# Joint attention block on one core: the image values multiplied key tile by key tile, narrow products in one bank, fourth token tile last

## The chip, the cores and the metric

The kernel runs on one core of a Trainium2 chip. The metric is the device time of one execution in microseconds (us); lower is better. A core has five engines that run side by side and wait for each other through semaphores: TensorE (matmuls; PE in the profile, its weight loads PEld), VectorE (DVE), ScalarE (ACT), GpSimd (POOL) and SyncE (SP), whose queue issues most of the loads (DMAs).

## What is computed

A joint attention block over 2 batches of 256 image tokens and 32 text tokens, width D = 1152, bfloat16. Cut to what matters here (the text side has the same form with its own weights):

```python
mod = (silu(c) @ wmod_img).reshape(B, 6, 1, D)
sh, sc, ga = mod[:, 0], mod[:, 1], mod[:, 2]
h = layernorm(x_img) * (1 + sc) + sh
q, k, v = split(h @ wqkv_img)
p = softmax(concat(qt, q) @ concat(kt, k).T * D ** -0.5)
out = x_img + ga * ((p @ concat(vt, v))[image rows] @ wo_img)
```

## The kernel before, in words

The 512 image tokens are four tiles of 128 rows (`NIT`, two to a batch, `TPB`), and D is nine key tiles of 128 (`KT`). The order of the work on every engine is the order in which the program is written (`tc.manual_schedule()`), so a wait of one instruction holds all that stand behind it on its engine. PSUM has eight banks: seven in the pool `ps_mm`, which are reused in turn, and one in `ps_sm`.

The part that the change rewrites is the value stage, from the first scale columns to the first q product:

- **Loads** (lines 92 to 118), all from SyncE's queue. The scale weights `w_sc_i` come in four chunks of columns, the value weights `w_v_i` in chunks of key tiles, both cut as `KC` says: (0,2), (2,4), (4,6), (6,9). The order is x tiles 0 and 1, scale chunk 0, x tile 2, value chunk 0, x tile 3, then scale and value chunks by turns, key tile 6 and key tiles 7 and 8 of the values on their own, then the shift and q weights in thirds (`K3`).
- **Normalising** (lines 164 to 180): VectorE's statistics of a tile, ScalarE's square root, VectorE's normalised rows `xn_i`.
- **Transposes** (`x_transposes`, line 193): nine per tile on TensorE into two PSUM tiles; ScalarE copies them to `hT_i` (`evac_low`, `evac_high`, lines 202 and 205) or, for the key tiles whose scale is known by then, scales them on the way (`evac_scaled`, line 198).
- **Scale** (`mod_scale`, line 210): 18 or 27 two-column matmuls per chunk, to which one engine adds 1 (line 219 or 221). `apply_mod` then multiplies `hT_i` in place by VectorE (0, line 229), GpSimd (1, line 234) or ScalarE (2, line 238).
- **Value products without the shift** (`v_part`, line 250). Each tile has two 512-wide halves, each with a bank of its own, and a 128-wide rest. `v_block` takes units and chunks by turns; seven of the eight halves are done so. The eighth is done behind them (line 401), and the rests last, two tiles to a bank (`v_rest`, line 350). `evac` empties a bank by VectorE and ScalarE in turn (lines 159 and 161).
- **Shift** of the image rows: `rows_for_cols` makes strips of the shift (lines 374 and 378), `select_cols` turns them into columns (390, 392), `cols_out` copies them out (395, 397), `apply_mod` adds them to `hT_i` after the value products have read it. The first 18 of the narrow rests stand in front of `select_cols`, the other 18 behind it.

What the values lack is put right later: VectorE multiplies the value weights by the shift (`shift_products`, lines 446 and 448), which goes through `shift_high`, `shift_low` (461) and `shift_strip` (468, 471).

Behind it, `qk_img` (line 486) makes q and then k for all 512 image tokens in 512-wide products: the first three column tiles as a group with the key tile as the outer loop, each later one on its own. Hooks put other work between them; in k these are the text side's normalising, its strips, its columns (`all_cols`, line 526), transposes (539) and the sums on VectorE (540, 542) that the text products (552) wait for. Then come scores, softmax, the attention output and the output projection (821).

Of the kernel before, what the change touches and what calls it, by code (L numbers as in the profile page):

```python
# [8 lines left out]
ACT = mybir.ActivationFunctionType  # L9
# [5 lines left out]
def kernel(  # L15
# [54 lines left out]
    def w_view(src):  # L70
        return src.rearrange("(kt p) n -> p kt n", p=P)
# [20 lines left out]
    def load_x(i):  # L92
        nc.sync.dma_start(x_i[:, i, :], xi_t[:, i, :])  # L93

    def load_sc(ch):
        k0, k1 = KC[ch]
        nc.sync.dma_start(w_sc_i[:, :, k0 * P:k1 * P], w_view(wmod_img)[:, :, D + k0 * P:D + k1 * P])

    def load_v(ch):
        k0, k1 = KC[ch]  # L100
        nc.sync.dma_start(w_v_i[:, k0:k1, :], w_view(wqkv_img)[:, k0:k1, 2 * D:3 * D])

    load_x(0)
    load_x(1)
    load_sc(0)
    load_x(2)
    load_v(0)
    load_x(3)
    for ch in range(1, len(KC)):
        load_sc(ch)  # L110
        if ch < len(KC) - 1:
            load_v(ch)
# [69 lines left out]
    xn_i = act.tile([P, NIT, D], bf, tag="A")  # L182
    hT_i = act.tile([P, KT, B * NI], bf, tag="Bt")

    mod_i = const.tile([P, 2 * KT, B], f32, name="mod_img")

    def x_transposes(i, n0=5):
        tps = (ps_mm.tile([P, n0, P], bf, tag="mm", name="tp"),
               ps_mm.tile([P, KT - n0, P], bf, tag="mm", name="tp") if n0 == 5 else
               ps_sm.tile([P, KT - n0, P], bf, tag="sm", name="tp"))  # L190
        for kt in range(KT):
            tp = tps[0][:, kt, :] if kt < n0 else tps[1][:, kt - n0, :]
            nc.tensor.transpose(tp, xn_i[:, i, kt * P:(kt + 1) * P], ident[:])  # L193
        return tps + (n0,)

    def evac_scaled(i, tps, n):
        for kt in range(n):
            nc.scalar.activation(hT_i[:, kt, i * P:(i + 1) * P], tps[0][:, kt, :], ACT.Identity,  # L198
                                 scale=mod_i[:, KT + kt, i // TPB:i // TPB + 1])

    def evac_low(i, tps, n):
        nc.scalar.copy(hT_i[:, n:tps[2], i * P:(i + 1) * P], tps[0][:, n:tps[2], :])

    def evac_high(i, tps):
        nc.scalar.copy(hT_i[:, tps[2]:KT, i * P:(i + 1) * P], tps[1][:])

    def mod_cols(wt, out_ps, j0, j1):
        for j in range(j0, j1):
# [1 line left out]
                nc.tensor.matmul(out_ps[:, j - j0, :], lhsT=wt[:, kt, j * P:(j + 1) * P], rhs=sT[:, kt, :],  # L210
                                 start=(kt == 0), stop=(kt == KT - 1))

    def mod_scale(ch, eng, own=True):
        k0, k1 = KC[ch]
        pool, tag = (ps_sm, "sm") if own else (ps_mm, "mm")
# [25 lines left out]

    vacc = {}

    def v_part(i, half, ch):
        k0, k1 = KC[ch]
        if ch == 0:
            vacc[i, half] = ps_mm.tile([P, VW], f32, tag="mm", name=f"va{i}{half}")
        ps = vacc[i, half]
        for kt in range(k0, k1):
            nc.tensor.matmul(ps[:], lhsT=hT_i[:, kt, i * P:(i + 1) * P], rhs=w_v_i[:, kt, half * VW:(half + 1) * VW],  # L250
                             start=(kt == 0), stop=(kt == KT - 1))
        if k1 == KT:
            evac(v_i[:, i, half * VW:(half + 1) * VW], ps[:])


    def v_block(units, chs):
        for ch in chs:
            for (i, half) in units:
                v_part(i, half, ch)

    warm(4)
    silu_c()
# [3 lines left out]
    def stats_of(i, k0, k1):  # L266
        lns[i] = ln_stats(x_i[:, i, :], P, k0, k1, lns.get(i))
# [10 lines left out]
    std_of(1)  # L278
    out_of(0)
    mod_scale(0, "act")  # L280
    tp0 = x_transposes(0)
    evac_scaled(0, tp0, 2)
    out_of(1)
    warm(1)
    tp1 = x_transposes(1, KT - 1)
    stats_of(2, 0, NCH)
    evac_scaled(1, tp1, 2)
    evac_low(0, tp0, 2)
    std_of(2)
    evac_high(0, tp0)  # L290
    evac_high(1, tp1)
    stats_of(3, 0, 1)
    out_of(2)
    v_block([(0, 0), (0, 1), (1, 0), (1, 1)], [0])
    evac_low(1, tp1, 2)
    tps = x_transposes(2, KT - 1)
    stats_of(3, 1, NCH)
    evac_scaled(2, tps, 2)
    std_of(3)
    mod_scale(1, "dve", own=False)  # L300
    for n, kt in enumerate(range(*KC[1])):
        apply_mod(kt, 0, 2, False, n)
    evac_low(2, tps, 2)
    evac_high(2, tps)
    v_block([(2, 0), (2, 1)], [0])
    out_of(3)
    for kt in range(*KC[1]):
        apply_mod(kt, 2, 3, False, 0)
    v_block([(0, 0), (0, 1)], [1])
    tps = x_transposes(3, KT - 1)  # L310
    evac_high(3, tps)
    evac_scaled(3, tps, 4)
    evac_low(3, tps, 4)
    v_block([(1, 0), (1, 1)], [1])
    mod_scale(2, "dve")
    for kt in range(*KC[2]):
        apply_mod(kt, 0, 2, False, 0)
        apply_mod(kt, 2, 4, False, 1)
    v_block([(2, 0), (2, 1)], [1])
    v_block([(3, 0)], [0, 1])  # L320
    v_i = act.tile([P, NIT, D], bf, tag="A")
    SEVEN = [(i, half) for i in range(NIT) for half in range(2)][:7]
    for (i, half) in SEVEN[:5]:
        v_part(i, half, 2)
    mod_scale(3, "dve")
    for b in range(B):
        for n, kt in enumerate(range(*KC[3])):
            apply_mod(kt, b * TPB, (b + 1) * TPB, False, (n + b) % 3)
    for (i, half) in SEVEN[5:]:
        v_part(i, half, 2)  # L330
    for (i, half) in SEVEN:
        v_part(i, half, 3)
# [5 lines left out]
    v_t = act.tile([P, VW], bf)  # L338
    v_t8 = act.tile([NTT, P], bf)
# [6 lines left out]
    def v_rest(i0, i1):  # L346
        ps = ps_mm.tile([P, TPB, P], f32, tag="mm")
        for kt in range(KT):
            for i in range(i0, i1):
                nc.tensor.matmul(ps[:, i - i0, :], lhsT=hT_i[:, kt, i * P:(i + 1) * P], rhs=w_v_i[:, kt, NM:D],  # L350
                                 start=(kt == 0 and i == i0), stop=(kt == KT - 1 and i == i1 - 1))
        return ps

    def v_rest_out(i0, i1, ps):
        evac(v_i[:, i0:i1, NM:D], ps[:])

    NGG = 4
    RC = 2 * P
# [40 lines left out]
    ps = ps_mm.tile([P, VW], f32, tag="mm")  # L399
    for kt in range(KT):  # L400
        nc.tensor.matmul(ps[:], lhsT=hT_i[:, kt, 3 * P:4 * P], rhs=w_v_i[:, kt, VW:NM], start=(kt == 0), stop=(kt == KT - 1))  # L401
    evac(v_i[:, 3, VW:NM], ps[:])
# [12 lines left out]
    w_k_i = load_w(wqkv_img, D, K3)  # L415
    w_sh_t = load_w(wmod_txt, 0)
# [57 lines left out]
        evac(g_sb[:], gps[:], "act")  # L474
        return g_sb

    def qk_img(wq, blk, hooks):

        groups = [(0, 3)] + [(j, j + 1) for j in range(3, KT)]
        for (j0, j1) in groups:  # L480
            if j0 in hooks:
                hooks[j0]()
            pss = [ps_mm.tile([P, B * NI], f32, tag="mm", name="qkps") for _ in range(j0, j1)]
            for kt in range(KT):
                for j in range(j0, j1):
                    nc.tensor.matmul(pss[j - j0][:], lhsT=wq[:, kt, j * P:(j + 1) * P], rhs=hT_i[:, kt, :],  # L486
                                     start=(kt == 0), stop=(kt == KT - 1))
# [36 lines left out]
        nc.scalar.activation(junk[:], eps_t[:], ACT.Exp)  # L524

    def all_cols():
        ctp = ps_sm.tile([P, 2, NCOL + B], f32, tag="sm")
        for k, rows in enumerate((strips["tsh"], strips["tsc"])):
            select_cols(rows, ctp[:, k, :])
        for k in range(2):  # L530
            cols_out(mod_t[:, k, :, :], ctp[:, k, :], float(k))

    def txt_transposes():
        pick = ident[:].rearrange("p (t r) -> p r t", r=P // NTT)[:, 0, :]
# [23 lines left out]
        all_cols()  # L558
        txt_transposes()

    qk_img(w_k_i, 1, hooks={3: txt_norm, 6: row_strips, 7: cols_and_transposes, 8: lambda: qk_txt(w_q_t, 0)})
    qk_txt(w_k_t, 1)


# [334 lines left out]
```

## Time and profile before

| | us |
|---|---|
| median of 3 runs | 116.68 (116.31 to 116.77) |
| the profiled execution | 116.51 |
| its span, first to last instruction | 114.5 |
| TensorE busy | 108.8 (95%) |
| VectorE, ScalarE, GpSimd busy | 75.0, 39.7, 27.6 |
| value stage, first scale column to first q product | 7.30 to 31.88 |
| q and k for the image, L486 | from 31.88, 162 products |
| DMA | 40.87 MB, 357 GB/s on average, about 410 from 20 us on |

In the timeline's rows the columns are: start, length, engine, line, operation, what it writes and reads, how often, and in brackets the engine's idle time before it with what ended it. Matmuls are pipelined, so that a row of them goes on for a little after the next row has started; the step from one start to the next is what a matmul costs. The granted clock of TensorE was 0.998 of full speed over the span.

### The profile page before, as it was taken

The page shows a single profiled execution, that of the slowest core. Times are in us where ns is not written, and L with a number is a line of the kernel's source. Part 1 is how long each engine was busy: PE and PEld are TensorE (multiplying, and loading weights), DVE is VectorE, ACT ScalarE, POOL GpSimd, SP SyncE. Part 2 cuts the span into 40 slices and gives each one's busy share as a digit, 9 for nine tenths or more (in the row PEclk, how much of TensorE's full clock was granted, in tenths as well). Part 3 has the DMA queues.
Part 4 walks back from the last instruction along what each step waited for, and adds up shares of the span by engine and source line. Part 5 has one row for each costly group of instructions (what it writes and reads, how often), then busy time and mean ns, then how long its engine had stood idle before and what let it go on. Part 6 is the DMA issues. An engine that isn't in the chain of part 4 may idle for free.

```text
span 114.5 us, 2919 instructions
## 1 busy us (share of the span) xinstructions
PE 108.8 (95%) x1230; PEld 64.7 (56%) x1230; DVE 75.0 (66%) x150; ACT 39.7 (35%) x93; POOL 27.6 (24%) x60
## 2 busy tenths in 40 slices
PE   5978999999999999999999999999999999999990
PEld 1344564544954444444447658787697566567560
DVE  1698920353399999999999760227656803998770
ACT  2729760342380630730009924025646700001000
POOL 7000103550050000000000051501540560899200
PEclk9999999999999999999999999999999999999999
DMA  3999999999999999999999999999999999962042
GB/s 81 315 346 355 372 383 398 411 412 411 408 407 412 405 416 401 412 412 411 412 411 411 410 405 411 404 389 399 411 408 403 409 410 398 388 273 102 26 163 69
DMA packets 22775, 40.87 MB, mean 357 GB/s; under 512 B 1311, under 2 KB 6571, under 8 KB 22763
## 3 DMA queue, kind: packets, MB, share of 16 engines
q1 hardware_dynamic: 21680, 39.64, 90.9%
q0 software_dynamic: 608, 0.88, 2.1%
q10 hardware_dynamic: 475, 0.18, 0.6%
q8 instruction: 9, 0.15, 0.5%
q14 instruction: 3, 0.02, 0.1%
HBM read 39.36 MB, written 1.34 MB: 356 GB/s over the span
## 4 chain that ended last, share of the span: by engine, by line
PE 87%; DMA 6%; SPq 2%; DVE 1%; issue 0%
PE qkps L486 31%; PE ps L821 16%; PE va L250 11%; DMA x_i<-in_x_img_dram 6%; PE aps L729 5%; PE ps L552 4%; PE sps L585 4%; PE gps L374 3%; PE ops L839 2%; PE ps L350 2%; PE ps L401 2%; PE ps L660 2%; SPq L93 1%; PE mps L210 1%; PE gps L794 1%; PE tp L193 1%
## 5 line engine op out<-in xcount | busy, mean ns | idle before, releaser
L486 PE MATMUL qkps<-hT_i,t 128*128 128x512 bf16 x162 | 35.6, 379 | 0.0
L486 PEld LDWEIGHTS <-t 128*128 128x128 bf16 x162 | 15.6, 98 | 18.3 <-issue 0.2
L448 DVE SCALAR_TENSOR_TENSOR sacc<-w_v_i,mod_img,sacc 128x1152 f32<-128x1152 bf16 x16 | 22.7, 1418 | 0.5
L821 PE MATMUL ps<-t,aT 128*128 128x384 bf16 x99 | 16.4, 326 | 0.0
L250 PE MATMUL va<-w_v_i,hT_i 128*128 128x512 bf16 x63 | 14.6, 379 | 0.5 <-DMA w_v_i<-in_wqkv_img_dram 0.5
L821 PEld LDWEIGHTS <-aT 128*128 128x128 bf16 x117 | 11.0, 98 | 6.8 <-issue 0.5
L827 DVE TENSOR_TENSOR tmp<-ps,gb 128x384 bf16<-128x384 f32 x11 | 6.1, 551 | 6.1 <-DMA gb<-mod_scratch 4.9
L250 PEld LDWEIGHTS <-hT_i 128*128 128x128 bf16 x63 | 5.8, 97 | 7.2 <-ACT hT_i L198 0.8
L805 POOL TENSOR_TENSOR w_og<-t,gb 128x384 bf16<-128x384 bf16 x9 | 8.8, 1006 | 4.5 <-PE ps L821 4.5
L507 POOL TENSOR_SCALAR svn<-svr 128x128 bf16<-128x128 bf16 x1 | 0.3, 298 | 32.8 <-ACT svr L156 32.8
L168 DVE BATCH_NORM_STATS2 stats<-x_i 128x6 f32<-128x384 bf16 x12 | 5.9, 543 | 2.9 <-DMA x_i<-in_x_img_dram 2.9
L436 ACT ACTIVATE qT<-qkps 128x512 bf16<-128x512 f32 x9 | 4.9, 596 | 6.4 <-PE qkps L486 6.4
L452 ACT CAST shi<-sacc 128x1152 bf16<-128x1152 f32 x2 | 2.3, 1152 | 13.7 <-DVE sacc L448 13.7
L142 PE MATMUL wps<-wz 128*128 128x512 bf16 x16 | 5.6, 499 | 1.2 <-DVE wz L127 1.2
L234 POOL TENSOR_SCALAR hT_i<-hT_i,mod_img 128x256 bf16<-128x256 bf16 x5 | 2.5, 510 | 15.9 <-ACT rstd L175 9.2
L742 DVE TENSOR_SCALAR aT<-aps,sv 128x288 bf16<-128x288 f32 (+2 forms) x11 | 4.3, 457 | 1.9 <-PE aps L729 1.9
L552 PEld LDWEIGHTS <-t 128*128 128x128 bf16 x162 | 4.9, 98 | 0.7 <-issue 0.5
L156 DVE CAST kT<-qkps 128x512 bf16<-128x512 f32 x3 | 2.1, 686 | 4.7 <-PE qkps L486 4.7
L552 PE MATMUL ps<-hT_t,t 128*128 128x64 bf16 x162 | 5.0, 193 | 0.0
L828 DVE TENSOR_TENSOR o<-tmp,x_i 128x384 bf16<-128x384 bf16 x11 | 4.7, 428 | 0.4
L744 ACT ACTIVATE aT<-aps,sv 128x288 bf16<-128x288 f32 (+2 forms) x11 | 4.0, 468 | 2.2 <-PE aps L729 2.2
L729 PE MATMUL aps<-pT,v_i 128*128 128x288 bf16 (+2 forms) x44 | 4.8, 264 | 0.0
(166 smaller groups left out, 148.0 us busy)
## 6 DMA issues: line engine op xcount, KB each, us to landing
t<-in_wmod_txt_dram SPq DMA_DIRECT2D x3, 2592.0 KB, 21.9
t<-in_wqkv_img_dram SPq DMA_DIRECT2D x6, 864.0 KB, 13.1
t<-in_wqkv_txt_dram SPq DMA_DIRECT2D x2, 2592.0 KB, 18.4
t<-in_wmod_img_dram SPq DMA_DIRECT2D x3, 864.0 KB, 11.6
w_home<-in_wmod_img_dram SPq DMA_DIRECT2D x1, 2592.0 KB, 14.7
t<-in_wqkv_txt_dram SPq DMA_DIRECT2D x3, 864.0 KB, 14.2
t<-in_wo_img_dram SPq DMA_DIRECT2D x1, 2592.0 KB, 17.8
t<-in_wo_txt_dram SPq DMA_DIRECT2D x3, 864.0 KB, 15.6
```

Of the source, the lines that this page charges most:

```text
L142: nc.tensor.matmul(ps[:], lhsT=wz[:, 0:P], rhs=wz[:], start=True, stop=True)
L168: nc.vector.bn_stats(stats[0:np_, k, :], x_ap[:, k * CH:(k + 1) * CH])
L250: nc.tensor.matmul(ps[:], lhsT=hT_i[:, kt, i * P:(i + 1) * P], rhs=w_v_i[:, kt, half * VW:(half + 1) * VW], start=(kt == 0), stop=(kt == K ...
L436: nc.scalar.mul(out_ap, in_ap, SCALE)
L448: nc.vector.scalar_tensor_tensor(saccs[b][:], w_v_i[:, kt, :], ap, saccs[b][:], op0=ALU.mult, op1=ALU.add)
L486: nc.tensor.matmul(pss[j - j0][:], lhsT=wq[:, kt, j * P:(j + 1) * P], rhs=hT_i[:, kt, :], start=(kt == 0), stop=(kt == KT - 1))
L552: nc.tensor.matmul(ps[:, j - j0, :], lhsT=wq[:, kt, j * P:(j + 1) * P], rhs=hT_t[:, kt, :], start=(kt == 0), stop=(kt == KT - 1))
L729: nc.tensor.matmul(bank[:, off:off + c1 - c0], lhsT=lhsT, rhs=rhs, start=(first[id(bank)] == n), stop=(final[id(bank)] == n))
L805: nc.gpsimd.tensor_mul(w_og[:, dt, 0:CH], w_o_i[:, dt, NG0:D], gb[:, B - 1, NG0:D])
L821: nc.tensor.matmul(ps[:, 0:cw], lhsT=aT[:, dt, t0:t0 + P], rhs=rhs, start=(dt == DTS[0]), stop=(dt == DTS[-1]))
L827: nc.vector.tensor_mul(tmp[:, 0:cw], ps[:, 0:cw], gb[:, b, cs])
L828: nc.vector.tensor_add(o[:, cs], tmp[:, 0:cw], x_i[:, i, cs])
```

## The change

- Value weights are loaded one key tile to a DMA (`load_v`), key tiles 7 and 8 still together. The fourth x tile's load moves to the place before the last scale chunk.
- `x_transposes` becomes `x_heads` (the first two key tiles; those of tiles 0 and 1 share a bank) and `x_tails` (the other seven). ScalarE scales the heads, key tile by key tile; the tails are copied by ScalarE, three key tiles of tile 1 by VectorE. The filler matmul `warm(1)` goes.
- `v_part` becomes `v_wide` and `v_narrow`. The narrow products of all four tiles share one bank, `van`, from the start, and stand between the wide ones; `v_row` does both halves of one tile and one key tile.
- The first three tiles' products follow the value rows as they come. The fourth tile's statistics, rows and transposes come late (`last_transposes`, VectorE scales on the way out), and its products come last. Its second half runs across `select_cols`, where the rests stood.
- `xn_i` shares the space of q, no longer that of `v_i`.
- q's first group has five column tiles, k's still three.
- The text columns go to two PSUM tiles; those of the shift are copied by ScalarE (`cols_copy`), those of the scale by VectorE, first.

The diff, cut to its core:

```diff
     def load_v(ch):
-        k0, k1 = KC[ch]
-        nc.sync.dma_start(w_v_i[:, k0:k1, :], w_view(wqkv_img)[:, k0:k1, 2 * D:3 * D])
+        for kt in range(*KC[ch]):
+            nc.sync.dma_start(w_v_i[:, kt:kt + 1, :], w_view(wqkv_img)[:, kt:kt + 1, 2 * D:3 * D])
...
     load_v(0)
-    load_x(3)
     for ch in range(1, len(KC)):
+        if ch == len(KC) - 1:
+            load_x(3)
         load_sc(ch)
...
+    def x_heads(tiles):
+        tp = ps_mm.tile([P, len(tiles), H, P], bf, tag="mm", name="tph")
+        for n, i in enumerate(tiles):
+            for kt in range(H):
+                nc.tensor.transpose(tp[:, n, kt, :], xn_i[:, i, kt * P:(kt + 1) * P], ident[:])
+        return tp
...
+    def x_tails(i):
+        pool, tag = (ps_mm, "mm") if i < TPB else (ps_sm, "sm")
+        tp = pool.tile([P, KT - H, P], bf, tag=tag, name="tp")
+        for kt in range(H, KT):
+            nc.tensor.transpose(tp[:, kt - H, :], xn_i[:, i, kt * P:(kt + 1) * P], ident[:])
+        return tp
...
+    def v_narrow(i, k0, k1):
+        if i == 0 and k0 == 0:
+            vacc["n"] = ps_mm.tile([P, NIT, P], f32, tag="mm", name="van")
+        for kt in range(k0, k1):
+            nc.tensor.matmul(vacc["n"][:, i, :], lhsT=hT_i[:, kt, i * P:(i + 1) * P], rhs=w_v_i[:, kt, NM:D],
+                             start=(i == 0 and kt == 0), stop=(i == NIT - 1 and kt == KT - 1))
+
+    def v_row(i, kt):
+        v_wide(i, 0, kt, kt + 1)
+        v_wide(i, 1, kt, kt + 1)
+
+    def last_transposes(k0, k1):
+        i = NIT - 1
+        b = i // TPB
+        tp = ps_sm.tile([P, k1 - k0, P], bf, tag="sm", name="tp")
+        for kt in range(k0, k1):
+            nc.tensor.transpose(tp[:, kt - k0, :], xn_i[:, i, kt * P:(kt + 1) * P], ident[:])
+        nc.vector.tensor_mul(hT_i[:, k0:k1, i * P:(i + 1) * P], tp[:],
+                             mod_i[:, KT + k0:KT + k1, b:b + 1].to_broadcast([P, k1 - k0, P]))
...
     out_of(1)
-    warm(1)
...
+    heads = x_heads((0, 1))
+    tails = [x_tails(i) for i in range(TPB)]
     stats_of(2, 0, NCH)
+    for kt in range(H):
+        for i in range(TPB):
+            head_scaled(heads, i, i, kt)
+    tail_out(0, tails[0], H, H + 3)
     std_of(2)
+    tail_out(1, tails[1], H, H + 3, on_vector=True)
+    tail_out(0, tails[0], H + 3, KT)
+    tail_out(1, tails[1], H + 3, KT)
     out_of(2)
+    for kt in range(*KC[0]):
+        for i in range(TPB):
+            v_row(i, kt)
+    for i in range(TPB):
+        v_narrow(i, *KC[0])
+    head2 = x_heads((2,))
+    tail2 = x_tails(2)
+    mod_scale(1, "dve", ps_mm, "mm")
...
+    v_wide(2, 0, *KC[0])
+    v_narrow(2, *KC[0])
+    v_wide(2, 1, *KC[0])
...
+    for kt in range(*KC[1]):
+        for i in range(TPB):
+            v_row(i, kt)
     mod_scale(2, "dve")
...
+    for i in range(TPB):
+        v_narrow(i, *KC[1])
+    for kt in range(*KC[1]):
+        v_row(2, kt)
+    v_narrow(2, *KC[1])
+    stats_of(3, 0, NCH)
+    std_of(3)
+    out_of(3)
+    k0, k1 = KC[2]
+    for i in range(3):
+        v_row(i, k0)
+    for i in range(TPB):
+        v_row(i, k0 + 1)
+    v_row(2, k0 + 1)
+    v_narrow(0, k0, k1)
     mod_scale(3, "dve")
...
+    for i in range(1, 3):
+        v_narrow(i, k0, k1)
+    last_transposes(0, KT - 1)
+    k0 = KC[3][0]
+    for i in range(3):
+        v_row(i, k0)
+        v_narrow(i, k0, k0 + 1)
+    last_transposes(KT - 1, KT)
+    for i in range(3):
+        for half in range(2):
+            v_wide(i, half, k0 + 1, KT)
+        v_narrow(i, k0 + 1, KT)
+    v_wide(3, 0, 0, KT)
+    v_narrow(3, 0, KT)
...
     shr = rows_for_cols(w_sh_i, "shr")
     cps = ps_sm.tile([P, NCOL + B], f32, tag="sm")
-    v_rest_out(TPB, NIT, v_rest(TPB, NIT))
+    v_wide(3, 1, 0, 5)
     select_cols(shr, cps)
     cols_out(mod_i[:, 0:KT, :], cps, 0.0)
-    vr = v_rest(0, TPB)
+    v_wide(3, 1, 5, KT, out=False)
...
-    v_rest_out(0, TPB, vr)
+    v_wide_out(3, 1)
+    evac(v_i[:, :, NM:D], vacc["n"][:])
...
-    qk_img(w_q_i, 0, hooks={5: lambda: shift_high(0)})
+    qk_img(w_q_i, 0, 5, hooks={5: lambda: shift_high(0)})
...
-        ctp = ps_sm.tile([P, 2, NCOL + B], f32, tag="sm")
-        for k, rows in enumerate((strips["tsh"], strips["tsc"])):
-            select_cols(rows, ctp[:, k, :])
-        for k in range(2):
-            cols_out(mod_t[:, k, :, :], ctp[:, k, :], float(k))
+        ctps = (ps_mm.tile([P, NCOL + B], f32, tag="mm", name="ctp"), ps_sm.tile([P, NCOL + B], f32, tag="sm", name="ctp"))
+        for ctp, rows in zip(ctps, (strips["tsh"], strips["tsc"])):
+            select_cols(rows, ctp)
+        cols_out(mod_t[:, 1, :, :], ctps[1], 1.0)
+        cols_copy(mod_t[:, 0, :, :], ctps[0])
```

More of the change, by code (lines that the diff above doesn't have):

```diff
@@ L180, in ln_apply, with head_scaled, tail_out @@
         nc.vector.tensor_scalar(out_ap, x_ap, mv[0:np_, 0:1], rstd[0:np_, :], op0=ALU.subtract, op1=ALU.mult)
-    xn_i = act.tile([P, NIT, D], bf, tag="A")
     hT_i = act.tile([P, KT, B * NI], bf, tag="Bt")
+    v_i = act.tile([P, NIT, D], bf, tag="A")
+    v_t = act.tile([P, VW], bf)
+    v_t8 = act.tile([NTT, P], bf)
+    xn_i = act.tile([P, NIT, D], bf, tag="Q")
     mod_i = const.tile([P, 2 * KT, B], f32, name="mod_img")
[L187 to L205, printed above, removed]
+    H = KC[0][1]
+    def x_heads(tiles):
[4 more added lines that the diff above has]
+        return tp
+    def head_scaled(tp, n, i, kt):
+        nc.scalar.activation(hT_i[:, kt, i * P:(i + 1) * P], tp[:, n, kt, :], ACT.Identity,
+                             scale=mod_i[:, KT + kt, i // TPB:i // TPB + 1])
+    def x_tails(i):
[4 more added lines that the diff above has]
+        return tp
+    def tail_out(i, tp, k0, k1, on_vector=False):
+        (nc.vector.tensor_copy if on_vector else nc.scalar.copy)(hT_i[:, k0:k1, i * P:(i + 1) * P], tp[:, k0 - H:k1 - H, :])
     def mod_cols(wt, out_ps, j0, j1):
@@ L211, in mod_cols, with mod_scale @@
                                  start=(kt == 0), stop=(kt == KT - 1))
[L213 removed]
+    def mod_scale(ch, eng, pool=ps_sm, tag="sm"):
         k0, k1 = KC[ch]
[L215 removed]
         mps = pool.tile([P, KT, B], f32, tag=tag)
@@ L242, with v_wide @@
     vacc = {}
-    def v_part(i, half, ch):
-        k0, k1 = KC[ch]
-        if ch == 0:
+    def v_wide(i, half, k0, k1, out=True):
+        if k0 == 0:
             vacc[i, half] = ps_mm.tile([P, VW], f32, tag="mm", name=f"va{i}{half}")
@@ L251, in v_part, with v_wide_out @@
                              start=(kt == 0), stop=(kt == KT - 1))
[L252 to L259, printed above, removed]
+        if k1 == KT and out:
+            v_wide_out(i, half)
+    def v_wide_out(i, half):
+        evac(v_i[:, i, half * VW:(half + 1) * VW], vacc[i, half][:])
+    def v_narrow(i, k0, k1):
[15 more added lines that the diff above has]
+                             mod_i[:, KT + k0:KT + k1, b:b + 1].to_broadcast([P, k1 - k0, P]))
     warm(4)
@@ L344 @@
     pxs = [act.tile([P, 2, B, NT], bf, name=f"px_{q}") for q in range(TPB)] + [act.tile([P, 2, B, NT], bf, name="px_t")]
[L346 to L355, printed above, removed]
     NGG = 4
@@ L397, in cols_out, with cols_copy @@
         nc.vector.tensor_scalar_add(dst[:, KT - 1, :], cps[:, NCOL:NCOL + B], add)
[L399 to L402, printed above, removed]
+    def cols_copy(dst, cps):
+        nc.scalar.copy(dst[:, 0:KT - 1, :].rearrange("p (g c) b -> p c g b", c=2),
+                       cps[:, 0:NCOL].rearrange("p (c g b) -> p c g b", c=2, b=B))
+        nc.scalar.copy(dst[:, KT - 1, :], cps[:, NCOL:NCOL + B])
     shr = rows_for_cols(w_sh_i, "shr")
     cps = ps_sm.tile([P, NCOL + B], f32, tag="sm")
-    v_rest_out(TPB, NIT, v_rest(TPB, NIT))
+    v_wide(3, 1, 0, 5)
     select_cols(shr, cps)
     cols_out(mod_i[:, 0:KT, :], cps, 0.0)
-    vr = v_rest(0, TPB)
+    v_wide(3, 1, 5, KT, out=False)
     SHE = ((0, 2), (0, 1), (2, 0), (0, 2), (1, 0), (2, 0), (0, 2), (1, 0), (2, 0))
@@ L475, in shift_strip, with qk_img @@
         return g_sb
-    def qk_img(wq, blk, hooks):
-        groups = [(0, 3)] + [(j, j + 1) for j in range(3, KT)]
+    def qk_img(wq, blk, jg, hooks):
+        groups = [(0, jg)] + [(j, j + 1) for j in range(jg, KT)]
         for (j0, j1) in groups:
```

54 lines of the change are left out of this document (10 added, 44 removed).

## The prediction

> **What bounds the kernel now.** I read the chain of work that ended last first, then TensorE's timeline, then the timelines of the queue and engines that feed it.
>
> From the profile page, the chain by engine:
>
> ```profile
> PE 87%; DMA 6%; SPq 2%; DVE 1%; issue 0%
> ```
>
> TensorE carries 87% of the chain; the rest is the first loads and the last store. So the end moves only by TensorE's own work and by gaps between its matmuls. Its timeline shows the few gaps (start, length, what, and in brackets the idle time before it):
>
> ```profile
> 7.30 0.61 PE L210 MATMUL mps<-sT,w_sc_i 128*128 128x2 bf16 x18 [0.79 <-DMA w_sc_i<-in_wmod_img_dram]
> 7.85 0.68 PE L193 MATMUL tp<-ident,xn_i 128*128 128x128 bf16 x9
> 8.36 0.38 PE L142 MATMUL wps<-wz 128*128 128x512 bf16 x1
> 8.58 0.67 PE L193 MATMUL tp<-ident,xn_i 128*128 128x128 bf16 x9
> 9.72 1.89 PE L250 MATMUL va<-w_v_i,hT_i 128*128 128x512 bf16 x8 [0.48 <-DMA w_v_i<-in_wqkv_img_dram]
> 11.68 0.68 PE L193 MATMUL tp<-ident,xn_i 128*128 128x128 bf16 x9
> ...
> 20.24 0.82 PE L210 MATMUL mps<-sT,w_sc_i 128*128 128x2 bf16 x27
> ...
> 31.88 29.30 PE L486 MATMUL qkps<-hT_i,t 128*128 128x512 bf16 x135
> ```
>
> Matmuls are pipelined: a row's length runs past the step to the next start. Steps, from rows: 0.216 us for a 512-wide matmul (135 in 29.14 on the chain), 0.056 for a 128-wide one or a transpose (L350: 18 in 1.17, less 0.22 of tail, over 17), 0.025 for a modulation column (27 in 0.82, less 0.16, over 26). The value stage runs from 7.30 to 31.88, 24.58 us. Its work is 72 wide (15.55), 36 narrow and 36 transposes (4.03), 81 columns (2.03), the shift strip with its switches (28.44 to 29.79, 1.35), select (0.08) and one filler matmul (0.22): 23.26. Only 1.32 us is waiting, 0.64 of it before 9.72 and 0.23 before 11.68. From 31.88 on every step is back to back, but for one place:
>
> ```profile
> 66.72 0.82 DVE L540 TENSOR_TENSOR hT_t<-tpt,mod_txt 128x320 bf16<-128x320 f32 x2
> 67.58 0.76 DVE L542 TENSOR_TENSOR hT_t<-hT_t,mod_txt 128x576 bf16<-128x576 bf16 x1
> ```
>
> TensorE's nine wide matmuls from 66.38 are through at 68.32 by the step; the text products (L552) start at 68.48, after VectorE's sum at 68.34. That is 0.16 us.
>
> The loads, from SyncE's queue (issue, length of the issue; first line the fourth x tile, last line the fourth scale chunk, 864 KB, 8.7 us to landing by the page, so 20.0):
>
> ```profile
> 3.47 0.47 SPq L93 DMA_DIRECT2D x_i<-in_x_img_dram  x1
> ...
> 11.29 0.47 SPq L97 DMA_DIRECT2D w_sc_i<-in_wmod_img_dram  x1
> ```
>
> **The value stage after the change, step by step.** It removes the filler (0.22), so 23.04 us of work is left: with no wait it would end at 30.34. I walk TensorE's new order with the steps above.
>
> - Scale columns 7.30 to 7.77, two transposes of tile 0 at 7.85. Tile 1's wait for its normalised rows: L180 at 7.90 + 0.58, start 8.54. Lost: 0.57, where the filler stood. The other 16 run to 9.44.
> - ScalarE scales the four heads from 8.92 (steps 0.27, as L198). The first single value row (128 of 256 rows of the old chunk, which landed at 2.99 + 6.7 = 9.7) is in at about 9.0, the second at 9.7, so the 8 wide products run 9.44 to 11.17 and not from 9.72; 4 narrow to 11.39.
> - Third tile: ScalarE's root now stands behind four heads and a copy (10.40, was 10.17); normalised at 10.93 + 0.58; transposes at 11.57. Lost: 0.18. The new VectorE copy of 384 (L159, 384 wide: 0.56) ends at 10.65, under that root. Then 9 transposes, 18 columns to 12.53, a wait of 0.05 for ScalarE's scaled heads, and 12 wide, 2 narrow to 15.28.
> - Next 18 columns to 15.74, then 16 wide and 8 narrow to 19.64. The fourth x tile went from before to behind two scale chunks and four value rows. So these land up to 0.7 us earlier (288 KB; the first two x tiles land 0.67 apart), x itself near 16.6; all ahead of need.
> - **The fourth scale chunk.** As many bytes stand ahead of it in the queue as before, so it lands at 20.0 again; TensorE comes for it at 19.64, not 20.24. Lost: 0.43. What was won at the start is given back here.
> - 27 columns to 20.75, 4 narrow to 20.97. The fourth tile's transposes take the bank that VectorE's scale sum reads: 20.88 for the last column, then 0.04 and 0.16 (L219): 21.15. Lost: 0.18. Eight transposes, 6 wide, 3 narrow to 23.07.
> - The last transpose needs the bank after a new VectorE multiply of 1024 elements from 21.81. From the nearest rows, L540 (320: 0.49) and L827 (384: 0.55): 0.92 to 1.2 ns per element, 1.15 to 1.35 us. Were all of it hidden it would cost 0; I take 1.25, so 23.12 and 0.08 lost.
> - Then 12 wide, 6 narrow, 9 wide, 9 narrow, strip, 5 wide, select, 4 wide: 31.95. The shift chain (select, VectorE, ScalarE, first q product) took 30.86 to 31.88, 1.03 us, under 18 narrow products; now it has four wide ones (0.89 with the select's step): 0.14 lost. **q starts at 32.09, +0.21.**
>
> The skill's page "VectorE: DVE Perf Modes" (The perf-mode tier table) gives a two-tensor operation that reads PSUM one element per cycle; its formula of (elements + 151) at 0.96 GHz makes the multiply 1.22 us, an estimate that the bounds from L540 and L827 contain. This is the Trainium skill's figure; the sum stands without it.
>
> **The narrow products in one bank.** 36 as before, but now between wide ones. A weight load's row is 97 ns against the 56 ns step, so a narrow one could cost up to 0.04 more, 1.5 us in all. Columns follow each other every 25 ns with a load of 96 each; of four returns to wide products in the old order (12.76, 15.04, 16.36, 20.92) one cost 0.11 and three nothing. I take 0. Below 0 is excluded: the work is the same.
>
> **Group of five in q.** 81 wide products either way. Weights' third chunk is needed after 30 products and not 18; it landed at 35.1 against 35.8, so nothing waited and nothing is won. Five evictions at 0.5 each end by 44.3; the next bank reuse is at 45.7: 0.
>
> **Text columns on ScalarE.** Two VectorE rows (0.09 + 0.08 by their starts, 66.45 to 66.63) leave the chain, the sum's end moves up 0.15: TensorE gains 0.15 of its 0.16. ScalarE has room (0.51 idle before 66.16).
>
> **VectorE's backlog.** Its last value eviction grows from 256 to 512 wide (0.33 to 0.60 by the starts), so the shift products start about 0.4 later, 0.2 against TensorE. Their last part is ready at 63.30 and read at 63.64: 0.3 of cover, so 0, and 0 to 0.1 if the cover is gone.
>
> **Sum.** +0.21 - 0.15 = +0.06. The profiled execution took 116.51 (span 114.5 and 2.0 around it): 116.6. The three runs shown have their median, 116.68, 0.17 above it: I say 116.7.
>
> **Rivals.**
> - *Split loads cost.* Three more DMAs are issued, at 0.43 to 0.47 each on SyncE: 1.3 us. It decides from the moment the fourth scale chunk lands after 20.02; each tenth later is a tenth lost, up to 118.0. Against: SyncE is held 2.8 to 3.3 us at L101, which means a full queue, and DMA runs at 340 to 410 GB/s. For: the chunk is now the tightest load. The Trainium skill, "DMA: Bandwidth & Descriptors" (Anatomy of one DMA, written for GpSimd's path), has about 2.0 us fixed per DMA; in series that would be 6 us. Two x tiles landing 0.67 apart show that in a queue it overlaps. Chance 0.15.
> - *Mixed shapes or the fourth tile's chain.* A return from narrow to wide at 0.11, 11 times, or the narrow loads at 0.04: 1.2 to 1.5, so 117.9. Or the fourth x tile lands after 18.2, from where its statistics, root, normalising (2.9 us together) miss 21.15: at 18.9, 117.4. Chance 0.13.
> - *The fourth chunk lands early* (0.4), the multiply and the shift chain hide (0.2): 116.0, faster. Against: its queue is no shorter. Chance 0.15.
> - *The text columns do nothing*: +0.15, 116.85, within the forecast.
>
> **Numbers.** Forecast 0.57, all within 0.5% (0.58 us, about what a measurement can tell from no change). Slower 0.15 + 0.13 = 0.28; faster 0.15. The range, 116.0 to 117.5, takes in the early chunk and the lower half of the slower cases.
>
> **What would show it.** A wait for w_sc_i before the 27 columns (0.4); tile 1's transposes at 8.54; single value rows landing in pairs about 0.7 apart; no added step at narrow products; q at 32.1; the text products 2.51 us long right behind the wide ones. It is wrong if that chunk lands over 0.5 away from 20.0, or if any wait over 0.3 stands elsewhere on TensorE.

## The result, and the profile after

The changed kernel takes 115.81 us (median of 18 runs, 115.60 to 116.45) against 116.62 us for the kernel before, timed beside it in 18 runs (115.95 to 117.09): a ratio of 0.9942, 95% interval 0.9926 to 0.9959. It is faster by 0.58%, 0.7 us by the ratio and 0.8 between the medians. The forecast was 116.7 and no measurable change; 115.81 lies below its range.

The profiled execution of the changed kernel took 115.73 (span 113.9, around it 1.86), that of the kernel before 116.51 (span 114.5, around it 2.05). The chain that ended last, by engine, in the profile after:

```profile
PE 90%; DVE 4%; DMA 3%; issue 1%
```

TensorE still carries it. Its timeline in the value stage (start, length, what):

```profile
7.49 0.59 PE L217 MATMUL mps<-sT,w_sc_i 128*128 128x2 bf16 x18
7.95 0.27 PE L197 MATMUL tph<-ident,xn_i 128*128 128x128 bf16 x2
8.44 0.29 PE L197 MATMUL tph<-ident,xn_i 128*128 128x128 bf16 x2 [0.22 <-DVE xn_i L181]
...
9.34 1.89 PE L255 MATMUL va<-w_v_i,hT_i 128*128 128x512 bf16 x7
11.07 0.39 PE L267 MATMUL van<-w_v_i,hT_i 128*128 128x128 bf16 x4
11.39 0.28 PE L197 MATMUL tph<-ident,xn_i 128*128 128x128 bf16 x2
...
19.33 0.28 PE L267 MATMUL van<-w_v_i,hT_i 128*128 128x128 bf16 x2
19.65 0.83 PE L217 MATMUL mps<-sT,w_sc_i 128*128 128x2 bf16 x27
20.34 0.38 PE L267 MATMUL van<-w_v_i,hT_i 128*128 128x128 bf16 x4
20.73 0.61 PE L279 MATMUL tp<-ident,xn_i 128*128 128x128 bf16 x8
...
31.55 3.61 PE L514 MATMUL qkps<-hT_i,t 128*128 128x512 bf16 x16
```

SyncE's issues of the fourth x tile and the fourth scale chunk, now one behind the other:

```profile
10.73 0.43 SPq L93 DMA_DIRECT2D x_i<-in_x_img_dram  x1
11.21 0.43 SPq L97 DMA_DIRECT2D w_sc_i<-in_wmod_img_dram  x1
```

The chunk is issued 0.08 earlier than before (11.29), and its last packet ends at 19.32 instead of 19.68. The prediction counted to the semaphore that tells TensorE of the landing, which comes 0.3 later: 19.60, before 20.02.

Read the timeline against the walk of the prediction. The wide products start at 9.34, no longer at 9.72. The two narrow ones of 19.33 are through by the step at 19.44, and the 27 columns start at 19.65: a wait of 0.21 for the fourth scale chunk, where 0.43 was forecast. q starts at 31.55, 0.33 ahead of before (31.88) and 0.54 ahead of the forecast (32.09).

VectorE's text rows (start, length, what):

```profile
66.24 0.82 DVE L568 TENSOR_TENSOR hT_t<-tpt,mod_txt 128x320 bf16<-128x320 f32 x2
67.17 0.76 DVE L570 TENSOR_TENSOR hT_t<-hT_t,mod_txt 128x576 bf16<-128x576 bf16 x1
```

TensorE's nine wide products ahead of the text products start at 66.05, these at 68.07: 2.02 apart, before 2.10. So 0.08 of the forecast 0.15 is won here. From there to TensorE's last matmul nothing more changes: it ends at 110.95 instead of 111.35, 0.40 earlier.

That is half of the 0.78 between the two executions. The other half comes after TensorE. From its last matmul to the last DMA packet both take 1.48. From that packet to the end of the span before takes 1.64, after 1.44 (0.20 less), and around the span lie 2.05 and 1.86 (0.19 less). SyncE's rows in the trace show the first of these. It closes the program by waiting for one DMA semaphore after another (times at which its waits come through; "last" is the one for the last store):

```
before: 112.93, last 113.19, 113.26, 113.32, 113.38, 113.44, 113.50, 113.56, drain 113.62
after:  112.10, 112.56, last 112.79, 112.85, 112.91, 112.97, drain 113.04
```

There are nine such waits, each 0.06 when its DMA has landed. In the trace the queue's DMAs take eight of the semaphores in rotation, so three more DMAs move the last store from the third wait to the sixth. Three waits are then past already: 0.18.

### The profile page after: what moved, and what is told of

The parts are those of the page before. It is cut to its first block, busy times and chain, and to the rows that moved or that the text cites. A ratio compares the mean times of both kernels' runs of the same rounds, so it can differ in the third digit from the quotient of the medians.

```text
span 113.9 us, 2913 instructions
## 1 busy us (share of the span) xinstructions
PE 109.0 (96%) x1221; PEld 65.2 (57%) x1229; DVE 76.2 (67%) x150; ACT 37.2 (33%) x87; POOL 27.4 (24%) x60
## 4 chain that ended last, share of the span: by engine, by line
PE 90%; DVE 4%; DMA 3%; issue 1%
PE qkps L514 31%; PE ps L849 16%; PE va L255 13%; PE aps L757 5%; PE ps L580 4%; PE sps L613 4%; PE gps L400 3%; DMA x_i<-in_x_img_dram 3%; DVE stats L169 2%; PE van L267 2%; PE ops L867 2%; PE ps L688 2%; PE mps L217 1%; PE gps L822 1%; PE tp L208 1%; DVE xn_i L181 1%
## 5 line engine op out<-in xcount | busy, mean ns | idle before, releaser
L255 PE MATMUL va<-w_v_i,hT_i 128*128 128x512 bf16 x68 | 16.8, 379 | 0.2
L255 PEld LDWEIGHTS <-hT_i 128*128 128x128 bf16 x72 | 6.4, 97 | 5.5
L143 PE MATMUL wps<-wz 128*128 128x512 bf16 x15 | 6.4, 600 | 1.2 <-DVE wz L128 1.2
L240 POOL TENSOR_SCALAR hT_i<-hT_i,mod_img 128x128 bf16<-128x128 bf16 (+1 forms) x5 | 2.1, 435 | 15.6 <-DVE mod_img L225 15.6
L160 DVE CAST v_i<-va 128x512 bf16<-128x512 f32 x5 | 3.4, 688 | 2.5 <-PE va L255 2.4
## 6 DMA issues: line engine op xcount, KB each, us to landing
t<-in_wqkv_img_dram SPq DMA_DIRECT2D x6, 864.0 KB, 13.5
```

Of the source, the lines that this page charges most:

```text
L143: nc.tensor.matmul(ps[:], lhsT=wz[:, 0:P], rhs=wz[:], start=True, stop=True)
```

## The experiments

All times of runs are medians, and each ratio is to runs of the kernel before that were timed beside it. Names with a_ are edits of the changed kernel, names with b_ of the kernel before. In the table: end of the last packet of the fourth scale chunk, start of the 27 columns, start of q, last packet to end of the span, time around the span (median over the runs), time, ratio.

| kernel | chunk | columns | q | closing | around | us | ratio, 95% |
|---|---|---|---|---|---|---|---|
| before | 19.68 | 20.24 | 31.88 | 1.64 | 2.08 to 2.19 | 116.62 | 1 |
| changed | 19.32 | 19.65 | 31.55 | 1.44 | 1.83 | 115.81 | 0.9942 [0.9926, 0.9959] |
| a_again | 19.10 | 19.63 | 31.52 | 1.44 | 1.93 | 115.75 | 0.9911 [0.9877, 0.9945] |
| a_x3_early | 19.19 | 19.57 | 31.47 | 1.44 | 1.87 | 115.99 | 0.9958 [0.9939, 0.9977] |
| a_text_dve | 19.28 | 19.61 | 31.51 | 1.44 | 1.93 | 115.84 | 0.9945 [0.9926, 0.9964] |
| a_group3 | 19.32 | 19.66 | 31.57 | 1.44 | 1.86 | 115.92 | 0.9953 [0.9930, 0.9976] |
| a_chunk0 | 19.24 | 19.52 | 31.42 | 1.44 | 1.90 | 115.75 | 0.9913 [0.9882, 0.9944] |
| a_pairs | 19.48 | 19.87 | 31.77 | 1.64 | 2.12 | 116.50 | 1.0003 [0.9979, 1.0026] |
| a_pairs_again | 19.45 | 19.83 | 31.74 | 1.64 | 2.17 | 116.56 | 0.9992 [0.9966, 1.0018] |
| a_pairs_plus3 | 19.72 | 20.11 | 32.02 | 1.45 | 1.90 | 116.09 | 0.9953 [0.9926, 0.9981] |
| a_plus3 | 19.86 | 20.21 | 32.11 | 1.26 | 1.80 | 115.64 | 0.9911 [0.9883, 0.9938] |
| a_plus5 | 19.15 | 19.55 | 31.45 | 1.70 | 1.77 | 115.87 | 0.9948 [0.9925, 0.9971] |
| a_fetch_late2 | 18.62 | 21.80 | 33.70 | 1.44 | 1.90 | 117.95 | 1.0126 [1.0098, 1.0155] |
| a_fetch_late3 | 19.38 | 19.74 | 31.65 | 1.44 | 1.89 | 115.87 | 0.9951 [0.9929, 0.9973] |
| b_split | 19.67 | 20.04 | 31.91 | 1.45 | 1.94 | 116.31 | 0.9982 [0.9960, 1.0004] |
| b_plus3 | 19.24 | 20.54 | 32.00 | 1.44 | 1.88 | 116.20 | 0.9962 [0.9939, 0.9984] |
| b_chunk0 | 20.05 | 20.30 | 32.25 | 1.64 | 2.17 | 116.51 | 0.9997 [0.9967, 1.0026] |

### The order of the loads, the single rows, the text columns

a_x3_early:

```diff
     load_v(0)
+    load_x(3)
     for ch in range(1, len(KC)):
-        if ch == len(KC) - 1:
-            load_x(3)
```

> The changed kernel with one thing undone: the fourth x tile is loaded right behind the first value rows, as before the change. The bytes ahead of the fourth scale chunk are the same. Theory A (the chunk landed 0.4 us earlier because of the new order of loads): it lands at about 20.0 again, TensorE waits about 0.55 us before the 27 columns instead of 0.2, and the time is 0.3 to 0.4 us above the changed kernel's 115.8. Theory B (the chunk's landing varies from one execution to the next, whatever the order): it lands anywhere from 19.5 to 20.0 and the time stays within 0.15 us of 115.8. Either way the value rows and scale chunks behind the moved tile land 0.7 us later than in the changed kernel, still ahead of TensorE.

The chunk ended at 19.19 and the columns began at 19.57, and q at 31.47: theory A is out. The median is 0.2 above the changed kernel's, with intervals that overlap, so no effect of the place of the fourth x tile is shown.

a_pairs, and a_pairs_again with the same edit:

```diff
-        for kt in range(*KC[ch]):
-            nc.sync.dma_start(w_v_i[:, kt:kt + 1, :], w_view(wqkv_img)[:, kt:kt + 1, 2 * D:3 * D])
+        k0, k1 = KC[ch]
+        nc.sync.dma_start(w_v_i[:, k0:k1, :], w_view(wqkv_img)[:, k0:k1, 2 * D:3 * D])
```

> The changed kernel with the value rows loaded two key tiles at a time again. Theory A' (the split into single rows is what brings the later chunks in earlier): the fourth scale chunk lands at about 20.0 and q starts 0.35 us later than in the changed kernel's profile (31.55), 116.15 in all. Theory B (the split does nothing for the chunk): the first wide products wait for the pair until about 9.6 instead of starting at 9.34, 0.25 us late, of which the wait of 0.2 before the 27 columns absorbs 0.2: 115.8 to 115.9.

> The changed kernel with value rows loaded in pairs, a second time, since its profile lost 0.22 us at q and its median 0.6 to 0.7. If the median is right, the ratio to before is 1.000 again and this profile shows the fourth scale chunk later than 19.8 (near 20.2); if the profile is right, the ratio comes to 0.996 to 0.997.

Both times the whole gain was gone, 0.6 to 0.7 us, while the profiles show q only 0.2 later. In a_pairs_again the first wide products wait for the pair:

```profile
9.80 1.89 PE L255 MATMUL va<-w_v_i,hT_i 128*128 128x512 bf16 x8 [0.21 <-ACT hT_i L201]
```

The row names ScalarE, but its first scaled head was done by 9.2; the pair landed at 9.66, and that is what ended the wait. The products start 0.46 after those of the changed kernel, of which 0.18 is left at the columns and 0.19 at q, since these wait for the chunk less. Neither theory gave 0.6; the closing, 1.64 again, and the 2.12 to 2.17 around the span held the rest, and this is what turned the search to the end of the program.

b_split is the single rows alone in the kernel before:

> The kernel before with one part of the change alone: the value rows in single loads. Its first product needs only the first row, its second the second row, so TensorE starts at 9.24 instead of 9.72 and waits for the second row until about 9.4 to 9.7. Theory A' (the split brings all later chunks 0.35 us earlier): the gain reaches q, which starts 0.3 us before 31.88: 116.3. Theory B (it doesn't): the second scale chunk still lands at 12.05, TensorE waits for it, and the gain at q is 0.0 to 0.15 us: 116.5 to 116.6. The rival of the prediction (three more loads cost SyncE time): the fourth scale chunk lands after 20.24 and the time is above 116.6.

TensorE reached the columns at 20.04 and lost it again behind them, on GpSimd's scaled rows:

```profile
20.04 0.83 PE L210 MATMUL mps<-sT,w_sc_i 128*128 128x2 bf16 x27
20.95 1.02 PE L250 MATMUL va<-w_v_i,hT_i 128*128 128x512 bf16 x4
22.20 4.48 PE L250 MATMUL va<-w_v_i,hT_i 128*128 128x512 bf16 x20 [0.24 <-POOL hT_i L234]
```

q stands at 31.91, so in this profile the early start alone wins nothing. The chunk's last packet ends at 19.67, as before the change (19.68), and earlier still in nearly all profiles of the changed kernel, so the rival of the split loads is out.

a_text_dve puts the text shift columns back (its other lines put both into one bank again):

```diff
...
-        cols_out(mod_t[:, 1, :, :], ctps[1], 1.0)
-        cols_copy(mod_t[:, 0, :, :], ctps[0])
+        for k in range(2):
+            cols_out(mod_t[:, k, :, :], ctp[:, k, :], float(k))
```

> The changed kernel with the text shift columns back on VectorE and in one bank. The prediction had this part at 0.15 us; the two profiles show TensorE's lead over the kernel before growing by only 0.08 us at the text products (0.33 at 66.05, 0.41 at 68.07). If the 0.15 is right the time is 115.95, if the 0.08 is right 115.9; the text products then start 2.17 or 2.10 us after the nine wide ones before them instead of 2.02. If ScalarE does nothing for it, 115.8.

The text products start 2.10 after the nine wide ones instead of 2.02. With ScalarE's columns the two multiplies (L568) do start 0.15 earlier against the wide products, as costed (0.19 after 66.05; with VectorE's 0.34 after 66.00), but the sum (L570) starts 0.11 after the second multiply's end instead of 0.03. ScalarE's copies were through by then (66.56). What is new ahead of the sum is one more semaphore instruction in VectorE's trace, at 67.10: the sum has two engines' semaphores to wait for, where it had one. So 0.08 is the size.

### Does the chunk's landing decide?

> The changed kernel once more, unchanged, for a second profile and a ratio on the chip on which the next kernels run. If the fourth scale chunk's landing is a property of the kernel, its wait before the 27 columns ends at 19.6 again and q starts at 31.5; if it varies between executions, by 0.2 us and more, the two profiles of one kernel differ by as much as those of different kernels did.

> The changed kernel with the 27 columns before the last value rows computed from the first three blocks of the scale weights, which have long landed, instead of the fourth chunk (so the last three scale blocks hold other values); all loads stay. TensorE then doesn't wait for the fourth chunk. If that wait is what is left and what spreads the changed kernel's times (115.60 to 116.45), the columns start at 19.44, the time is 0.2 to 0.4 us below the changed kernel's in the same call, and the spread shrinks; the next load due is the seventh value row, 20.4 against 21.2. If the chunk bounds nothing in a usual execution, the time is the same.

> The kernel before with the same edit: its 27 columns are computed from the first three scale blocks, which have landed, and all loads stay. In its profile the chunk landed at 20.02 and TensorE came at 20.24, so nothing is won: 116.5, if that execution was a usual one. If the chunk usually lands later than 20.24 in the kernel before, the time falls by as much, and the changed kernel's gain is partly a wait that its profile of before didn't show.

In a_again the chunk's last packet ended 0.22 earlier than in the first profile of the same kernel, but the first wide products started 0.12 later (9.46), TensorE came to the columns at 19.63 by itself, and q stands at 31.52. The other two have this edit:

```diff
-        mod_cols(w_sc_i, mps, k0, k1)
+        j0 = 0 if ch == 3 else k0
+        mod_cols(w_sc_i, mps, j0, j0 + k1 - k0)
```

Without the wait, a_chunk0's columns follow the narrow products at once:

```profile
19.41 0.28 PE L268 MATMUL van<-w_v_i,hT_i 128*128 128x128 bf16 x2
19.52 0.82 PE L217 MATMUL mps<-sT,w_sc_i 128*128 128x2 bf16 x27
```

q comes at 31.42, and the time is that of a_again: in a usual execution the wait is worth about 0.1 or less. b_chunk0 shows nothing either (0.9997); the kernel before was not held by the chunk. But the landing does vary from one profile to the next, and when it is late the changed kernel pays. The kernel before and its two variants with the same loads up to there have 19.68, 20.05 and 19.24. In a_plus3, whose loads up to there are those of the changed kernel:

```profile
19.35 0.28 PE L267 MATMUL van<-w_v_i,hT_i 128*128 128x128 bf16 x2
20.21 0.83 PE L217 MATMUL mps<-sT,w_sc_i 128*128 128x2 bf16 x27 [0.59 <-DMA w_sc_i<-in_wmod_img_dram]
...
32.11 1.24 PE L514 MATMUL qkps<-hT_i,t 128*128 128x512 bf16 x5
```

TensorE came at 19.46, as in the changed kernel, and waited 0.75 by its step, 0.54 more than the changed kernel's 0.21; q is 0.56 later (32.11 against 31.55). This execution took 116.03, where the median is 115.64. In all thirteen profiles of changed kernels q starts 11.89 to 11.91 after the columns, and in ten of them the columns start 0.33 to 0.40 after the chunk's last packet, as soon as it has landed. In a_again and a_fetch_late2 TensorE came later than that, and a_chunk0 doesn't need the chunk.

### The closing

> The kernel before with three more DMAs and nothing else: the key weights, first used some 10 us after they land, are loaded in six pieces instead of three. Theory C (part of the gain is the closing: SyncE waits for the DMA semaphores one after another, 0.06 us each, and three more DMAs move the last store's semaphore from the third of nine waits to the sixth): TensorE ends at 111.35 as before, the last packet to the end of the span takes 1.44 us instead of 1.64, and the time falls by 0.2 us for this alone, by up to 0.45 if what lies around the span (2.17 us in most runs of before, 1.9 in runs of the changed kernel) goes with it: 116.1 to 116.35. Theory D (the closing is chance, and the gain lies in the value stage alone): 116.5, closing 1.64.

> The changed kernel with the value rows in pairs (which lost all of the gain twice) and three DMAs added on the key weights, so that it has as many DMAs as the changed kernel. Theory C: the closing is 1.44 us again, what lies around the span about 1.9, and of the 0.7 us that the pairs lost, 0.2 to 0.45 come back: 116.1 to 116.3; q stays at 31.75. Theory A' (the single rows bring all of it by landing earlier): 116.5.

> The changed kernel with three more DMAs on the key weights: the last store's semaphore comes ninth of nine waits. Theory C: the closing falls from 1.44 to 1.26 us, the time to 115.6 (0.18 below the changed kernel), more if what lies around the span falls too. Theory D: 115.8.

> The changed kernel with five more DMAs on the key weights: eight more than before the change, so the last store's semaphore is the third of nine waits again. Theory C: the closing is 1.64 us again and the time 0.2 to 0.45 above the changed kernel's, 116.0 to 116.25, though the value stage is untouched (q at 31.5). Theory D: 115.8.

```diff
-    w_k_i = load_w(wqkv_img, D, K3)
+    w_k_i = load_w(wqkv_img, D, ((0, 2), (2, 4), (4, 6), (6, 7), (7, 8), (8, KT)))
```

(This is the edit of b_plus3 and a_plus3; a_pairs_plus3 has it beside that of a_pairs, and a_plus5 has eight pieces.) SyncE's last waits in three of them:

```
b_plus3: 112.81, 113.24, last 113.47, 113.54, 113.59, 113.66, drain 113.72
a_plus3: 113.11, last 113.35, drain 113.41
a_plus5: 112.44, last 112.70, 112.77, 112.83, 112.89, 112.95, 113.01, 113.10, drain 113.18
```

The closing came out as the rotation has it: 1.44, 1.45 and 1.26, and 1.70 where 1.64 was expected. b_plus3 has none of the change but its number of DMAs, and it is faster by 0.38% (0.16 to 0.61), 0.4 us, although TensorE ended later than before in its profile (111.64). b_split has the same number, and its 0.18% (0.40 faster to 0.04 slower) agrees with that or with nothing. a_pairs_plus3 is 0.4 to 0.5 us below the pairs without it, at a q that is 0.25 later. So theory C stands for the closing, and D is out. One half of C fell: what lies around the span doesn't go with the closing. It went down with the number of DMAs added: 2.08 to 2.19 with none, 1.83 to 1.94 with three, 1.80 with six, 1.77 with eight, so a_plus5 stayed at 115.87, below the 116.0 to 116.25 that was expected of it. What takes that time isn't in the span, and no run here shows it. a_plus3 has the lowest time of all, but its interval doesn't part it from the changed kernel.

### What holds the chunk back, and the group of five

The packets of the chunk (768 bytes, 36 ns each) in slices of 0.2 us give the mean number in flight, which I read as the DMA engines that carry it:

```
from             17.6 17.8 18.0 18.2 18.4 18.6 18.8 19.0 19.2 19.4
before             11    9    6    5    4    2    1    1    1    1
changed            15   11    5    2    1    1    1    1    1    0
a_again            10    8    5    3    3    3    3    1    0    0
a_fetch_late2      15   10    5    2    1    0    0    0    0    0
```

In the kernel before and in the changed one a single engine carries on alone; in a_again three do, to 19.0. The chunk's semaphore tells the same. Of its sixteen steps the fifteenth came at 19.00 and the last at 20.02 before the change, at 18.72 and 19.60 after it, at 18.64 and 18.96 in a_fetch_late2; in a_again the last three came at 19.29, 19.37 and 19.41. The page of the profile counts nine packets of the instruction queue (q8), 16 KB each; the first comes at 16.12 in before and 15.56 in the changed kernel, and takes 0.94 and 0.97. a_fetch_late2 and a_fetch_late3 were to move it:

```diff
-    warm(4)
+    warm(1)
     silu_c()
-    warm(11)
+    warm(0)
```

That is a_fetch_late2; a_fetch_late3 has warm(3) as its last line, and its warming matmuls are in f32.

> The changed kernel with one warming matmul at the start instead of fifteen: 28 instructions fewer on TensorE ahead of everything, so the 16 KB instruction packet comes about 28 instructions later, some 3 us of the value stage, at 18 to 18.8 instead of 15.5. Theory E (that packet, 0.94 us on one DMA engine, is what makes the fourth scale chunk late): the chunk's last packet ends near 18.7 instead of 19.1 to 19.3, TensorE begins the 27 columns without a wait, and q starts up to 0.2 earlier, unless TensorE, idle before 7.3, runs slower at first (its matmul steps after 7.3 tell). Theory F (the last engine is late for another reason): the chunk ends at 19.1 to 19.3 or later, wherever the packet stands.

> The same aim with TensorE kept busy: the fifteen warming matmuls are replaced by four in f32, which take longer each. If they are single instructions, the instruction packet moves behind the fourth scale chunk as in the kernel beside it; if they are several each, it stays near 15.5. Theory E: chunk's last packet near 18.7 where the packet comes after 18, q at 31.3 to 31.4, 115.6. Theory F: as in the changed kernel, 19.1 to 19.3, q at 31.5.

In a_fetch_late2 the packet came at 19.43, and the chunk's last packet ended at 18.62, with no engine left over, as theory E has it. It is the only profile with the packet behind the chunk, and the only one below 19.1. The trace doesn't name the engine of a packet, so that the late one is the one with the instruction packet is inferred. The price was elsewhere:

```profile
8.75 1.70 PE L208 MATMUL tp<-ident,xn_i 128*128 128x128 bf16 x14
10.24 3.46 PE L255 MATMUL va<-w_v_i,hT_i 128*128 128x512 bf16 x8
13.54 0.39 PE L267 MATMUL van<-w_v_i,hT_i 128*128 128x128 bf16 x4
```

Until about 13.5 a wide product steps every 0.427 us and a transpose every 0.107, twice as long as after it, and the page's clock row shows 9 throughout. The Trainium skill, "TensorE: Matmul & The Clock Gate" (Part 1: The HAM clock gate), gives just these two steps for an array that was idle, and some 3.4 us of work until it is fast; the steps agree, but the time was longer here: 5 us from the transposes at 8.56, 6 from the columns at 7.45. In a_fetch_late3 each f32 matmul shows as two records, the packet moved to 16.08 only, and the chunk ended at 19.38: it doesn't test the theory. The Trainium skill, "Runtime: NRT & Kernel Launch" (Terms), has the instruction memory refilled in blocks of 16 KiB; the packets' size here agrees.

E explains up to about 0.9 of lateness on one engine. It doesn't explain the three late ones of a_again, nor the last step of the semaphore 1.30 behind the fifteenth in a_group3 and 1.46 in b_chunk0, nor why the landing differs by 0.76 (19.10 to 19.86) among kernels that load alike. E is supported by one profile and is not all of it; the rest stays open.

> The changed kernel with the first query group of three columns again instead of five. The prediction costed the group of five at nothing, since the same 81 wide products run back to back in both: 115.8, and q's products take 29.1 us from first to last as with five. If the later need for the third piece of the query weights or the longer run of free banks is worth anything, the time is 0.1 us or more above that, with a gap on TensorE between 31.5 and 61.

q's image products start at 31.57 and the strip behind them at 60.80, 29.23 later; with five it is 31.55 and 60.78, the same. The group of five is worth nothing, as costed.

## Why the prediction was wrong

**The step that failed is the fourth scale chunk**: "so it lands at 20.0 again". One landing of one execution was taken as a property of the queue. It came at 19.60 in the changed kernel, and at 19.59 to 20.38 in three profiles that load like the kernel before, so whether the change itself brings it forward is not shown. The columns started at 19.65 and not at 20.07, and the rest of the stage followed: 0.42 of the 0.54 by which q came earlier. When the chunk does land late (20.16 in a_plus3), q starts at 32.11, and the walk said 32.09. So close a match is in part luck: the columns started 0.14 later than in the walk, and what follows them took 0.12 less. But the mechanism was right: TensorE waits for the chunk, and q follows 11.9 later. Its input was not. Its rival, "the fourth chunk lands early", was held down to 0.15 by "its queue is no shorter"; the bytes ahead don't fix a landing for which the last one to three of sixteen engines decide.

**The end of the program was left out of the sum.** The three more DMAs were priced only as a cost on SyncE's issue. They gave 0.20 in the closing and about 0.2 to 0.3 around the span. b_plus3 shows this alone at 0.4 us (0.2 to 0.7). Over all runs of b_plus3 and b_split together, 24 of them, the mean is 0.3 us (0.2 to 0.4) below that of the kernel before, so this is nearly half of the gain. That part doesn't belong to the value products at all.

The other steps, in order:

- Tile 1's transposes started at 8.44 (8.54 forecast). TensorE came to the columns at 19.44 (19.64). Third tile: ScalarE's root at 10.20 (10.40), VectorE's copy of 384 took 0.29 and not 0.56 (it reads bf16 from PSUM, the row taken for it f32); a wait of 0.10 there (the narrow products are through at 11.29, the transposes start at 11.39) instead of 0.18.
- Single rows landed 0.69 and 0.71 apart (0.7). x of the fourth tile landed at 17.56, not 16.6, and was normalised at 20.48, in time for 20.73.
- After the columns: wait for VectorE's sum 0.17 (0.18); multiply of 1024 elements 1.22 us (1.25), which cost 0.03 (0.08); shift chain 0.10 (0.14). 11.90 from columns to q where the walk has 12.02. Right in kind, each a little smaller.
- Narrow products between wide ones: steps of 0.05 to 0.06 and no added step at the returns (22.10 narrow, 22.15 wide). Nothing, as forecast.
- Text columns: 0.08 and not 0.15, for the wait on a second engine that the sum got.
- Group of five: nothing, as forecast. VectorE's backlog: the strip's read of the last part came 0.14 after the one before it instead of 0.11, so 0.03, within 0 to 0.1.

Together: value stage -0.33 (forecast +0.21), text -0.08 (-0.15), closing -0.20 and around the span -0.19 (not forecast): -0.80 by the parts, -0.78 between the profiled executions.

What the new order of products is worth by itself can be read from runs with as many DMAs. One kernel against one it is barely parted from noise: 0.9942 against 0.9982 (b_split, the same loads but for the fourth x tile) and 0.9962 (b_plus3); in pairs it has 0.9953. Taken together, the 24 runs of the changed kernel (a_again with them) have a mean span of 114.0, those of b_split and b_plus3 114.4 (difference 0.35, give or take 0.16), 111 runs of the kernel before 114.5. So about 0.4 us belongs to TensorE's work, and the rest to the number of DMAs. Single rows and new order belong together: b_split's q is no earlier than before (31.91), and in pairs the order brings q forward by 0.11 to 0.14 in two profiles, of which the times of 24 runs show nothing.

## What to carry to other kernels

Take a DMA's landing from one profile as one draw: put its spread into the sum, above all where the change turns a load that was just in time into one that is waited for. Walk to the very end of the program as well: here the order in which SyncE waits for its DMA semaphores and the time around the span were together worth nearly as much as the work on TensorE, and an edit that only changes the number of DMAs moves both. When a part that should matter little takes the whole gain with it (the pairs), compare the ends of the two traces before inventing a mechanism at the place of the edit.

## What was not expected of the hardware

- A packet of 16 KB of the instruction queue takes about 0.94 us, and a load that is spread over sixteen engines lands with its last engine: the chunk's last packet ended at 18.62 with that packet behind it, at 19.10 to 19.86 in the profiles of the changed kernel with it ahead. That the packet is the cause rests on the one profile.
- Semaphore waits at the end cost 0.06 us each even when their DMAs landed long ago: 1.64 to 1.70, 1.44 and 1.26 us of closing with the last store third, sixth and ninth.
- Leaving fourteen of fifteen warming matmuls out cost 2.1 us. Seven wide products at 0.427 instead of 0.216 and fourteen transposes at 0.107 instead of 0.056 make 2.2.
